# Values in uneven groups around the blocks of the second layer, and one load of v placed later

## The chip, the cores and the metric

The kernel runs on one core of one Trainium2 chip. What counts is the time of the whole execution on the device, in microseconds. Before the change it was 451.67 us, the median of 3 runs (449.34 to 451.85).

The engines are named as in the profile: PE multiplies matrices and writes PSUM, with PEld for the loads of its weights; DVE is VectorE, ACT is ScalarE, POOL is GpSimd, SP is SyncE, which here only issues transfers.

## The reference

Attention with a sigmoid in place of a softmax, and then a layer that works on a chosen part of the tokens. Batch 8, 12 heads, 448 tokens, head size 64, all float32:

```
scores = q @ k^T / 8 - log(448)
attn   = sigmoid(scores) @ v                     # per head
x      = attn of the 12 heads side by side       # (8, 448, 768)
score  = x @ w_gate
for each batch: top = the 128 tokens of highest score
    xe  = x[top]
    out = x;  out[top] = xe + sigmoid(score[top]) * (relu(xe @ w1) @ w2)
```

w1 is 768x1024 and w2 is 1024x768.

## The kernel before

**Steps and slots.** The 96 heads are worked on in 12 steps (s = 0 to 11) of 8 heads. A step has 7 slots (n = 0 to 6), and a slot is a share of the keys: n selects 2 times 32 tokens of keys for each of four head groups. In a slot, `slot` (L738) makes the scores of (s, n), and beside them values (scores times v) of earlier slots. The values run four slots behind: those of step s begin in slot 4 of step s and end in slot 3 of step s + 1.

**Units.** One call of `score(s, n, e, pr, out)` (L330) multiplies on the rows of the array that belong to pr: pr = 1 takes rows 64 to 127, pr = 0 takes rows 0 to 63. Two calls, e = 0 and 1, complete one tile PA[pr] of PSUM, and `squash` (L344) then makes its sigmoid on ACT. One call of `value(s, half, p, n)` (L358) multiplies the sigmoids of slot n with v and adds into the two banks PO[half]; half = 0 uses rows 0 to 63, half = 1 rows 64 to 127. The index p says which of the two banks takes which rows; for each half there are p = 0 and 1 and n = 0 to 6, 14 value units in a step. So a score unit of pr = 1 and a value unit of half = 0 use different rows of the array and run side by side, and likewise pr = 0 and half = 1. I call two units side by side a pair. PE starts its products in the order of the program.

**A plain slot** is, in order: score e0 pr1, two values of half 0, score e1 pr1, sigmoid of PA[1]; then score e0 pr0, two values of half 1, score e1 pr0, sigmoid of PA[0]. That is four pairs. `rounds` (L718) lists which values (p, u, w) stand in which slot; both halves take the same.

**The split slot.** One slot of each step, chosen by `split` (L728), has values of both p of one slot n: in the steps ahead of a block it is the last slot (i = 6, which is slot 3 of the next step). There the order is value half 0, `join(0)`, value half 1, `join(1)`, the four score units, value half 1, value half 0, and the two sigmoids. `join(x)` (L374) is two copies of one element on ACT into the banks PO[x]; the later values of the other p wait for them.

**Blocks.** Behind slot 3 of step s, `after` (L852) loads the next v (`load_v`, L133, four transfers on ACT's queue for s > 4) and calls `block(s)` (L680) for s = 4 to 11. A block moves the finished values out of PSUM (`takes`, DVE transposes, L389) and does the work of the second layer that is listed in `BLOCKS` (L650): "c" chooses the rows of a batch and issues their gather, "t" turns the gathered rows (L524 on PE, then the copies L526 and L527 and a small sigmoid L529 on ACT), and (m, pair, key) is one product of the first (m = 1, 24 records at L560) or second (m = 2, 8 records at L624) matrix, with its sums on DVE and ACT. The banks that these write are handed out in the order of the list `places`:

```
places = [PA[1][:, 0], PO[0][0], PO[0][1], PA[0][:, 0], PO[1][0], PO[1][1], PA[0][:, 0]]
```

A "t" takes two. Blocks 5, 7, 8, 10 and 11 end with a "t", whose second copy empties the seventh place, PA[0]. Block 5 is: choose batch 1, turn batch 0, two products of the first matrix, turn batch 1.

**The order of everything** is written out by hand; each engine works its own list in order, and waits where a tile is not ready. DVE's list holds, between blocks, the transposes of q and k, the gates (L397, L400), sums of weights (L208), and the ranking of tokens (L445, L448) with what follows it (L460, L469, L473).

**v** has one buffer for most steps, so a load of v can start only behind the last values of the step before. It is four transfers of 224 KB, one for each 32 rows; the value unit of half 0 needs the first two, that of half 1 the last two.

Of the kernel before, what the change touches and what calls it, by code (L numbers as in the profile page):

```python
# [17 lines left out]
def kernel(  # L18
# [20 lines left out]
    NF = 3  # L39
# [3 lines left out]
    NS = NQ // 2  # L43
    NU = 2 * NF + 1
# [27 lines left out]
    PA = [ps_a.tile([P, 2, 512], F32, name=f"a{n}") for n in range(2)]  # L72
# [60 lines left out]
    def load_v(s):  # L133


        if s >= NS:
            return
        if s in (1, 3):
            t = moe.tile([P, 6 * KH * P], F32, name="rows_t")[:, :4 * NU * Dh]
        else:  # L140
            t = vals.tile([P, 4 * NU * Dh], F32, name="raw_v")
        raw_v[s] = t = t.rearrange("p (h c) -> p h c", h=4)

        def block(x, r, n):
            return bass.AP(tensor=v.tensor,
                           offset=v.offset + (8 * s + 4 * x) * S * Dh + r * Dh,
                           ap=[[TB * Dh, TT], [S * Dh, 4], [1, n * Dh]])

        for m in range(4):
            y, odd = divmod(m, 2)  # L150
            rows = slice(m * TT, (m + 1) * TT)
            if s:
                (nc.scalar if s > 4 else nc.sync).dma_start(
                    out=t[rows], in_=block(y, odd * NU, NU))
            else:
                nc.sync.dma_start(out=t[rows, :, :NA * Dh], in_=block(y, odd * NA, NA))
                nc.sync.dma_start(out=t[rows, :, NA * Dh:],
                                  in_=block(1 - y, 2 * NA + 2 * odd, 2))
# [215 lines left out]
    def join(x):  # L374

        for t in PO[x]:
            nc.scalar.activation(t[Dh:Dh + 1, S:S + 1], bias_s[Dh:Dh + 1], AF.Copy)

    def takes(s, x):
        for pr in range(2):  # L380
            take(s, pr, x)
# [130 lines left out]
    def turn_rows(b, both):  # L512


        n = CAP
        p, odd = divmod(b, 2)
        if not odd:
            t = moe.tile([P, 6 * KH * P], F32, name="rows_t")
            pairs[p] = {"x": t.rearrange("p (m k n) -> p m k n", m=6, k=KH)}
        x = pairs[p]["x"]  # L520
        ps = [t.rearrange("p (k n) -> p k n", n=P) for t in both]
        for t in range(KD):
            a, i = divmod(t, KH)
            nc.tensor.transpose(ps[a][:, i, :n], st[b]["xe"][:n, t * P:(t + 1) * P],  # L524
                                iden[:n, :n])
        nc.scalar.activation(x[:, 2 * odd, :, :n], ps[0][:, :KH, :n], AF.Copy)  # L526
        nc.scalar.activation(x[:, 2 * odd + 1, :, :n], ps[1][:, :KH, :n], AF.Copy)  # L527
        st[b]["gate"] = moe.tile([P, 1], F32, name="gate", bufs=4)
        nc.scalar.activation(st[b]["gate"][:n], st[b]["picked"][:n], AF.Sigmoid)  # L529
        if not odd:  # L530
            return
        for dst, y, z in ((4, 2, 0), (5, 3, 4), (2, 3, 2)):
            nc.vector.tensor_tensor(out=x[:, dst, :, :n], in0=x[:, y, :, :n],
                                    in1=x[:, z, :, :n], op=ALU.subtract)
        pairs[p]["turned"] = True
        last_row(p)
# [143 lines left out]
    def block(s):  # L680

        places = [PA[1][:, 0], PO[0][0], PO[0][1], PA[0][:, 0], PO[1][0], PO[1][1], PA[0][:, 0]]
        work = BLOCKS.get(s, ())
        if work and work[0][0] == "c":
            chosen = choose(work[0][1], places.pop(0))
        takes(s - 1, 0)
        if work and work[0][0] == "c":
            fetch(*chosen)
            work = work[1:]
        takes(s - 1, 1)  # L690
        stores(s, NF)
        if s in FULL[::2]:
            gates(2 * s - 2)
        for item in work:
            if item[0] == "t":
                turn_rows(item[1], [places.pop(0) for _ in range(2)])
            elif item[0] == "c":
                fetch(*choose(item[1], places.pop(0)))
            else:
                finish(item, begin(item, places.pop(0)))  # L700
# [17 lines left out]
    def rounds(s):  # L718


        if s == 0:
            return [(0, 0, 1), (1, 0, 1), (1, 0, 1), (0, 0, 1), (0, 4, 5), (0, 1, 6), (1, 4, 5)]
        same = [(0, 0, 1), (1, 0, 1), (1, 2, 3), (0, 2, 3), (0, 4, 5)]
        if s + 1 in BLOCKS:
            return same + [(1, 4, 5), (1, 0, 6)]
        return same + [(0, 1, 6), (1, 4, 5)]

    def split(s, i):  # L728
        return i == (6 if s + 1 in BLOCKS else 5)

    def entries(s, i, half):

        p, u, w = rounds(s)[i]
        if s == 0 and i < 4 and (i < 2) == bool(half):
            u, w = 2, 3
        return (p, u), (p, w)

    def slot(s, n):  # L738


        if s == 0 and n < NF + 1:
            if n == NF:
                first_outs.close()
                open_outs()
            psc = PA if n % 2 else outs
            for e in range(2):
                for pr in (1, 0):
                    score(s, n, e, pr, psc[pr])
            for pr in (1, 0):
                squash(s, n, pr, psc[pr])  # L750
            return
        vs, i = (s, n - NF - 1) if n > NF else (s - 1, n + NF)
        if split(vs, i):
            one, two, u = rounds(vs)[i]
            for half in range(2):
                value(vs, half, one, u)
                join(half)
            for e in range(2):
                for pr in (1, 0):
                    score(s, n, e, pr, PA[pr])  # L760
            for half in (1, 0):
                value(vs, half, two, u)
            for pr in (1, 0):
                squash(s, n, pr, PA[pr])
            return
        for half in range(2):
            pr = 1 - half
            a, b = entries(vs, i, half)
            if s == 0 and n == NF + 1 and half == 0:
                value(vs, half, *a)  # L770
                value(vs, half, *b)
                score(s, n, 0, pr, PA[pr])
            else:
                score(s, n, 0, pr, PA[pr])
                value(vs, half, *a)
                value(vs, half, *b)
            score(s, n, 1, pr, PA[pr])
            if vs == 0 and half == 1 and i in (1, 3):
                join(1 if i == 1 else 0)
            squash(s, n, pr, PA[pr])  # L780
            if i == 6 and s not in BLOCKS:
                takes(vs, half)
# [69 lines left out]
    def after(s, n):  # L852

        if n == NF and s:
            odd = s in FULL[1::2]
            if s > 4:
                load_v(s)
            elif s < 4:
                load_v(s + 1)
            if s in BLOCKS:  # L860
                block(s)
            else:
                stores(s, n)
            if s == 2:
                gates(2 * s - 2)
            turn("q", 2 * s + 2)
            turn("k", 2 * s + 3)
            load("k", 2 * s + 4)
            turn("q", 2 * s + 3)
            if s not in FULL[::2]:  # L870
                gates(2 * s - 2)
            if s == FIRST:
                ranking(1)
            gates(2 * s - 1)
        for m, key, place in LENT.get((s, n), ()):
            lend(m, key, place)
        if s == 0:
            if n == 0:
                turn("k", 1)
                turn("q", 1)  # L880
                load("k", 2, 3)
                load("q", 2, 3)
            if n == 4:
                turn("k", 2, 3)
                load_v(1)
                load("k", 4)
            if n == 5:
                turn("q", 2, 3)
        if (s, n) in WEIGHTS:
            m, x = WEIGHTS[s, n]  # L890
            if x is None:
                load_left(m)
            else:
                load_held(m, x)
        for m, key in KEPT.get((s, n), ()):
            keep_sum(m, key)
        if (s, n) in MADE:
            make_sum(*MADE[s, n])
        for b in range(B - 1):
            full = FULL[b]  # L900
            if (s, n) == ((4, 0) if b == 1 else (full, 5 + b % 2)):
                spread(b)
            if (s, n) == RANKED[b]:
                ranking(b)
        if n != NF:
            stores(s, n)
# [63 lines left out]
```

## Time and profile before

| | |
|---|---|
| median of 3 runs | 451.67 us (449.34 to 451.85) |
| the profiled execution | 450.95 us |
| its span, first to last instruction | 449.1 us |
| PE busy | 437.2 us, 97% |
| DVE, ACT, POOL busy | 301.8, 191.0, 32.7 us |
| mean granted clock of PE | 0.989 |
| one score product (L339), one value product (L368) | 538 ns, 536 ns; eight run at a time |
| one sigmoid (L353) | 1007 ns |
| 24 products of the first matrix at full clock | 2.68 us |

Times in the trace count from the span's start. The products of PE overlap, so a sum of their durations says little; what a stretch takes is read from the starts. PE shows each float32 product of this kernel's slots as two records. A share of busy time near 100% does not mean that the array is full: a score unit alone on its rows keeps PE busy and half of the array empty.

### The profile page before, as it was taken

How to read it: one execution, taken by the hardware profiler on the slowest of the kernel's cores; microseconds unless marked ns; L12 is line 12 of the kernel's file. 1: busy time of each engine (PE TensorE's matmuls, PEld its weight loads, DVE VectorE, ACT ScalarE, POOL GpSimd, SP SyncE). 2: the span in 40 equal slices, each digit the busy share in tenths (PEclk: the TensorE clock that was granted, in tenths of full speed). 3: DMA queues.
4: the chain of work that ended last, by engine and by line, in shares of the span. 5: the costliest groups of instructions: out<-in, count | busy, mean ns of one | idle time of the engine just before them, and what ended most of it. 6: DMA issues, size and time to landing. Idle time of an engine off the chain costs nothing.

```text
span 449.1 us, 14350 instructions
## 1 busy us (share of the span) xinstructions
PE 437.2 (97%) x6374; PEld 259.9 (58%) x6374; DVE 301.8 (67%) x639; ACT 191.0 (43%) x257; POOL 32.7 (7%) x55
## 2 busy tenths in 40 slices
PE   8999999999989999999999999999999999999994
PEld 3456554444358568446447558636545749769952
DVE  4317277945954995966998785655795669883462
ACT  4766666665643641660661661462264330101100
POOL 7000000000001000100002000010000101001001
PEclk9999999999988999999999999999999999999998
DMA  8975737997571898679566499399864974611001
GB/s 242 257 239 132 259 86 141 233 222 177 163 210 43 181 325 218 178 203 312 165 225 159 131 249 191 84 265 227 223 229 85 203 224 64 118 36 72 1 0 70
DMA packets 112846, 76.80 MB, mean 171 GB/s; under 512 B 90304, under 2 KB 99136, under 8 KB 112784
## 3 DMA queue, kind: packets, MB, share of 16 engines
q1 hardware_dynamic: 106768, 61.55, 53.0%
q10 hardware_dynamic: 4032, 6.42, 6.2%
q0 software_dynamic: 1984, 7.91, 5.9%
q8 instruction: 50, 0.82, 0.8%
q14 instruction: 12, 0.10, 0.1%
HBM read 55.41 MB, written 20.46 MB: 169 GB/s over the span
## 4 chain that ended last, share of the span: by engine, by line
PE 86%; DVE 8%; ACT 2%; issue 2%; DMA 1%; ACTq 1%; POOLq 0%; DVEq 0%
PE a L339 27%; PE o L368 23%; PE o L624 12%; PE o L560 10%; PE a L560 7%; PE a L624 3%; DVE scr L448 1%; DVE scr L445 1%; ACT attn L353 1%; PE p L926 1%; ACT hidden L353 1%; DVE x_b L389 1%; DVE sums L473 1%; DVE spare L208 1%; DVE kT L321 1%
## 5 line engine op out<-in xcount | busy, mean ns | idle before, releaser
L339 PE MATMUL a<-qT,kT 32*64 32x448 f32 x2624 | 244.4, 538 | 0.6 <-DVE got L496 0.5
L353 ACT ACTIVATE attn<-a,bias_s 128x896 f32<-128x896 f32 x162 | 161.9, 1007 | 84.8 <-PE a L339 81.1
L368 PE MATMUL o<-attn,raw_v 32*64 32x448 f32 x2176 | 197.3, 536 | 0.1
L339 PEld LDWEIGHTS a<-qT,kT 32*64 32x64 f32 x2624 | 92.6, 131 | 96.8 <-ACT attn L353 57.3
L368 PEld LDWEIGHTS o<-attn,raw_v 32*64 32x64 f32 x2176 | 74.3, 131 | 31.3 <-issue 24.5
L389 DVE STREAM_TRANSPOSE x_b<-o 128x448 f32<-128x448 f32 x48 | 27.6, 620 | 55.3 <-PE o L368 32.5
L368 PE MATMUL o<-attn,rows_t 32*64 32x448 f32 x448 | 42.3, 537 | 0.1
L576 ACT ACTIVATE hidden<-hidden 128x512 f32<-128x512 f32 x12 | 7.5, 630 | 70.1 <-DVE hidden L573 70.1
L400 DVE TENSOR_REDUCE gate_p<-scr 128x14 f32<-128x448 f32 x48 | 29.8, 622 | 1.7
L573 DVE TENSOR_TENSOR hidden<-o,hidden 128x512 f32<-128x512 f32 x20 | 13.2, 687 | 25.4 <-PE o L560 25.2
L397 DVE TENSOR_TENSOR scr<-x_b,wg_b 128x448 f32<-128x448 f32 x48 | 29.4, 612 | 1.1
L321 DVE STREAM_TRANSPOSE kT<-raw_k 128x448 f32<-128x448 f32 x42 | 24.1, 612 | 8.2 <-PE o L368 4.5
L624 PE MATMUL o<-w_sb,hidden 128*128 128x384 f32 x80 | 27.4, 487 | 0.0
L635 DVE SCALAR_TENSOR_TENSOR xe<-o,gate,xe 128x384 f32<-128x384 f32 x36 | 20.5, 611 | 9.5 <-PE o L624 9.3
L313 DVE STREAM_TRANSPOSE qT<-qT 128x896 f32<-128x896 f32 x23 | 25.0, 1085 | 2.7 <-DMA qT<-in_q_dram 2.7
L560 PE MATMUL o<-rows_t,w_sb 128*128 128x128 f32 x192 | 23.2, 278 | 0.0
L526 ACT ACTIVATE rows_t<-o 128x384 f32<-128x384 f32 x7 | 3.4, 483 | 45.9 <-PE o L524 43.6
L560 PEld LDWEIGHTS o<-rows_t,w_sb 128*128 128x128 f32 x192 | 22.7, 196 | 0.3
L448 DVE SCALAR_TENSOR_TENSOR scr<-rep,who,earlier 128x448 f32<-128x448 f32 (+1 forms) x32 | 21.9, 683 | 1.4
L445 DVE TENSOR_SCALAR_CACHE_REDUCE scr<-rep,who 128x448 f32<-128x448 f32 (+1 forms) x32 | 21.5, 673 | 1.0
L368 PEld LDWEIGHTS o<-attn,rows_t 32*64 32x64 f32 x448 | 17.6, 131 | 6.4 <-issue 4.6
L624 PEld LDWEIGHTS o<-w_sb,hidden 128*128 128x128 f32 x80 | 14.7, 190 | 8.8
(114 smaller groups left out, 403.1 us busy)
## 6 DMA issues: line engine op xcount, KB each, us to landing
qT<-in_q_dram SPq DMA_DIRECT2D x24, 448.0 KB, 6.2
out_dram<-x_b SPq DMA_DIRECT2D x32, 336.0 KB, 8.6
raw_k<-in_k_dram SPq DMA_DIRECT2D x22, 448.0 KB, 5.3
spare<-sum SPq DMA_DIRECT2D x18, 384.0 KB, 5.2
raw_v<-in_v_dram ACTq DMA_DIRECT2D x28, 224.0 KB, 6.1
sum<-spare SPq DMA_DIRECT2D x8, 768.0 KB, 7.2
w_sb<-in_moe_w_dram SPq DMA_DIRECT2D x6, 768.0 KB, 7.6
rows_t<-in_v_dram SPq DMA_DIRECT2D x8, 224.0 KB, 5.9
```

What stands on the lines that cost most here:

```text
L313: nc.vector.transpose(heads["q", i], heads["q", i])
L321: nc.vector.transpose(kt[:, e], t[:, e].rearrange("p (a n) d -> p n a d", a=2))
L339: nc.tensor.matmul(out[y * Dh:(y + 1) * Dh, h % 2, :S], kt[d, e, r:r + 2].rearrange("d r t -> d (r t)"), qt[d, e], start=(e == 0), stop=(e ...
L353: nc.scalar.activation(a, psc[:, :, :S], AF.Sigmoid, bias=bias_s, scale=QK_SCALE)
L368: nc.tensor.matmul(PO[x][pr][j * Dh:(j + 1) * Dh, :S], raw_v[s][rows, 2 * pr + j, at:at + Dh], attn[s, pr, n][rows, j, :], start=((s, x, p ...
L389: nc.vector.transpose(x_tiles[b][:, :, 2 * g + pr, :], PO[x][pr][:, :S].rearrange("p (r t) -> p r t", t=TT))
L397: nc.vector.tensor_tensor(out=tmp, in0=x_tiles[b][:, :, hp, :], in1=wg_b[:, hp:hp + 1, :].to_broadcast([P, TB, TT]), op=ALU.mult)
L400: nc.vector.tensor_reduce(out=gate_parts[b][:, :, hp], in_=tmp, axis=AX.X, op=ALU.add)
L445: nc.vector.tensor_scalar(out=junk[:n], in0=rep[:n], scalar1=own, scalar2=0.0, op0=ALU.is_gt, op1=ALU.add, accum_out=above[:n, c:c + 1])
L448: nc.vector.scalar_tensor_tensor(out=junk[:n], in0=rep[:n], scalar=own, in1=earlier[:n, c, :], op0=ALU.is_equal, op1=ALU.mult, accum_out=l ...
L560: nc.tensor.matmul(ps[:, f, :n], w((t * FH + f) * P, P), x[:, t, :n], start=(t == 0), stop=(t == KH - 1))
L624: nc.tensor.matmul(ps[:n, :DH], h[:, t, :n], w(t * DH, DH), start=(t == 0), stop=(t == FH - 1))
```

## The change

It does four things. The first three hold for the values of steps 4 to 10, called `LATE`; the values of other steps are placed as before.

1. The two halves no longer take the same values in a slot. `LOW` and `HIGH` list them by slot, for half 0 and half 1.
2. The first two slots behind a block (slots 4 and 5) are written out in `first_slots`. In slot 4 the second score unit of PA[1] and the first of PA[0] stand side by side, in the second pair, so that PA[1] is complete after the second pair and PA[0] after the third, and the fourth pair holds two values. Half 0 has one value of each p there, with `join(0)` between.
3. The last slot before the next block is written out in `last_slot`, and replaces the split slot: its first pair holds two values, PA[1] is complete after the third pair and PA[0] after the fourth. Half 0 is finished after the second pair, half 1 after the fourth, with `join(1)` between its two values.
4. The four transfers of v for step 5 are issued in block 5 behind the row turn of batch 0 (behind L529 on ACT's queue) instead of ahead of the block.

The number of products, sigmoids, copies and transfers is the same, and so is the order on DVE, SP and POOL. The core of the diff:

```
@@ block(s)
             if item[0] == "t":
                 turn_rows(item[1], [places.pop(0) for _ in range(2)])
+                if item[1] == 0:
+                    load_v(s)
@@
+    LATE = range(min(BLOCKS), NS - 1)
+    LOW = {6: (1, 3, 4), 0: (0, 1, 2), 1: (1, 5, 6), 2: (0, 3, 4), 3: (0, 5, 6)}
+    HIGH = {6: (1, 0, 1), 0: (1, 2, 3), 1: (1, 4, 5), 2: (0, 4, 5)}
+
+    def first_slots(s, n):
+        def u(e, pr):
+            score(s, n, e, pr, PA[pr])
+
+        if n == NF + 1:
+            u(0, 1)
+            value(s, 0, 0, 0)
+            join(0)
+            u(1, 1)
+            u(0, 0)
+            squash(s, n, 1, PA[1])
+            value(s, 1, 0, 0)
+            u(1, 0)
+            squash(s, n, 0, PA[0])
+            value(s, 1, 0, 1)
+            value(s, 0, 1, 0)
+            return
+        u(0, 1)
+        value(s, 0, 1, 1)
+        value(s, 0, 1, 2)
+        u(1, 1)
+        squash(s, n, 1, PA[1])
+        u(0, 0)
+        value(s, 1, 0, 2)
+        value(s, 1, 0, 3)
+        u(1, 0)
+        squash(s, n, 0, PA[0])
+
+    def last_slot(s, n):
+        p, one, two = LOW[n]
+        value(s - 1, 1, 0, NU - 1)
+        value(s - 1, 0, p, one)
+        join(1)
+        score(s, n, 0, 1, PA[1])
+        value(s - 1, 0, p, two)
+        score(s, n, 1, 1, PA[1])
+        score(s, n, 0, 0, PA[0])
+        squash(s, n, 1, PA[1])
+        value(s - 1, 1, 1, NU - 1)
+        score(s, n, 1, 0, PA[0])
+        squash(s, n, 0, PA[0])
@@ entries(s, i, half)
+        if s in LATE:
+            p, u, w = (HIGH if half else LOW)[(i + NF + 1) % NU]
+            return (p, u), (p, w)
@@ slot(s, n)
-        if split(vs, i):
+        if vs in LATE and i < 2:
+            first_slots(s, n)
+            return
+        if vs in LATE and n == NF:
+            last_slot(s, n)
+            return
+        if vs not in LATE and split(vs, i):
@@ after(s, n)
-            if s > 4:
+            if s > 5:
                 load_v(s)
```

## The prediction

> **What bounds the kernel now.** TensorE does. The page's first row has PE busy 97% of the 449.1 us span, and the chain that ended last is 86% PE. So a change gains only where PE waits, where it runs without its partner, or where its clock is low. I read three views for that. First the page's slices, for the granted clock:
>
> ```profile
>
> ```
>
> One place inside the kernel, slices 12 and 13 of 11.2 us each, is below full. The waits of PE name what stands there:
>
> ```profile
> PE a L560 <- ACT rows_t L526: 1.5, 1, 1.5
> ```
>
> It is the longest wait of PE. The chain in order of time shows it (start, us, what), and from the next block a product of the same size:
>
> ```profile
> 129.09 0.39 ACTq L153
> ...
> 130.00 1.15 ACTq L153
> ...
> 131.81 0.50 ACT rows_t L526
> ...
> 132.36 5.49 PE a L560 x24
> ...
> 170.23 2.68 PE a L560 x24
> ```
>
> In the block of step 5, ScalarE issues the four transfers of v (L153, 129.09 to 131.63) ahead of the copy that PE needs (L526). Then 24 products take 5.49 us instead of 2.68. The windows give the reason (PE busy first, PEclk after the five engines):
>
> ```profile
> 131.00:132.00 1.00, 0.00 (x0) 0.00 (x0) 1.00 (x2) 0.19 (x1) 0.57 (x1) 0.86 1.08 245
> 132.00:133.00 1.00, 0.64 (x3) 0.65 (x4) 0.93 (x3) 0.77 (x3) 0.00 (x0) 0.50 1.09 232
> ...
> 138.00:139.00 1.00, 1.00 (x9) 1.00 (x8) 0.00 (x0) 0.48 (x1) 0.58 (x1) 0.72 0.00 0
> 139.00:140.00 1.00, 1.00 (x12) 1.00 (x11) 0.00 (x0) 0.00 (x0) 0.00 (x0) 1.00 0.40 108
> ```
>
> By the shares 0.86 and 0.72 the clock is half from 131.72 to 138.55, 6.83 us. PE works from 132.36, so half speed costs (138.55 - 132.36) / 2 = 3.1 us on top of the wait.
>
> **The units.** In the timeline a score unit is 8 records, a value unit 8, and one of each run side by side in 0.75 us; a slot is four such pairs, 3.02 us. I write t0 for the start of the last slot before a block and E for the first score behind it.
>
> **Last slot (blocks 5 to 11).** Before, it takes 3.85 us (159.84 to 163.69 in step 6), since scores and values run unpaired and one score waits. The weight loads show it:
>
> ```profile
> 160.63 0.18 PEld L339 LDWEIGHTS a<-qT,kT 32*64 32x64 f32 x4 [0.20 <-issue]
> 161.27 0.58 PEld L339 LDWEIGHTS a<-qT,kT 32*64 32x64 f32 x20 [0.46 <-ACT attn L353]
> ```
>
> After, four full pairs end at t0 + 3.1. But the block's first product writes PA[1], whose last score pair is now the third. A sigmoid starts 0.75 after its second round (159.47, then 160.21): t0 + 1.9 + 0.75 = 2.65; it takes 1.01, and PE follows 0.05 later: t0 + 3.70. So 0.15 is gained, not 0.75. The two small ScalarE copies that each new join adds to a slot (0.25 us by L377's 0.44 for four) stand ahead of a sigmoid; only a value a pair or more later waits for them, and before there were four per last slot. I cost them at nothing, at most 0.25 each.
>
> In blocks 9 and 11 the next wait, for VectorE's transposes of PO[0] (L389), also goes: PO[0] is complete after the second pair, so both transposes (0.65 and 0.61) end near t0 + 3.0. The next product starts at 3.70 + 0.36 (choice, 270.41 to 270.77) + 0.19 = t0 + 4.25, instead of 4.72 and 4.67: **-0.47 and -0.42**. Blocks 7 and 10 start with a product in PA[1]: **-0.15 each**. Blocks 6 and 8 gain nothing, because VectorE is late by itself. Its chain runs without a gap from 155.67, and from 213.53, to:
>
> ```profile
> 166.15 0.66 DVE x_b L389
> ...
> 166.85 0.61 PE o L482 x4
> ```
>
> and to 236.20 in block 8. Its order is not changed.
>
> **Block 5.** Before: t0 = 125.07, E = 141.51, so 16.44. After: choice at t0 + 3.70, for 0.91 (128.93 to 129.84); row turns at 4.61; the first copy 0.53 after them (213.32, 213.85 in block 7), at 5.14, for 0.49; PE 0.06 later at 5.70, not 7.29. Two products at 2.68 and six turns at 0.75 give E = t0 + 11.81 at full clock: **-4.63**, of which 3.1 is the clock.
>
> The moved step is four issues on ScalarE's queue, now behind L529 at about t0 + 6.15. They take 1.75 (four at 0.44) to 2.55 us. Behind them stands L579, wanted at t0 + 8.45; it is 0.25 late at most, and its reader comes 2.7 us later. No other queue is passed. What is new is when v lands. Before, the last piece lands 7.95 after the first issue (137.04); other blocks show 7.3 to 12.3. That is t0 + 13.4 to 18.4, wanted at E + 1.69 = 13.5. The lower end is 0, the upper 4.9. I take 0, because nothing but the gather was moving beside it before, and the 1.15 of the third issue included a wait for a weight that landed at 130.47, which is past by then.
>
> **First slots behind a block.** The first score of PA[0] moves from the third pair to the second, from E + 1.55 to E + 0.8. PA[0] is the last bank that a row turn used in blocks 5, 7, 8 and 10. Its copy ends at E + 0.65 in blocks 7 and 10: nothing. In blocks 5 and 8 a relu stands in front:
>
> ```profile
> 248.48 0.63 ACT L576 ACTIVATE hidden<-hidden 128x512 f32<-128x512 f32 x1 [2.88 <-DVE hidden L573]
> 249.02 0.47 ACT L526 ACTIVATE rows_t<-o 128x384 f32<-128x384 f32 x1
> 249.39 0.48 ACT L527 ACTIVATE rows_t<-a 128x384 f32<-128x384 f32 x1
> ```
>
> It ends at E + 1.63 (E = 248.24). The score starts at E + 1.69, its partner has gone alone, and one pair of the next slot loses its partner: the two slots last 6.95, against 3.24 + 3.02 before. **+0.7 in each of blocks 5 and 8.** Between, the groups only change which values stand in a slot; every slot has four pairs, and each value's sigmoid is at least a slot old: 0.
>
> **Sum.** -4.63 + 0.7 + 0.7 - 0.15 - 0.15 - 0.47 - 0.42 = -4.4. The profiled execution took 450.95 (span 449.1), so it would take 446.5. The median of the runs shown, 451.67, stands 0.7 above it, so I predict **447.2**. The lowest of them, 449.34, is 2.3 lower, which fits an execution without the half clock; from there the other terms, -1.3, give 448.0.
>
> **A rule on the clock.** The row: the slow stretch is 6.83 us, and in the 3.4 us ahead of it PE was still recorded busy for about 2.6 us (idle only from 130.9). [...] The row says that a thin window is enough, so 449.6 stays possible.
>
> **Rivals.**
> *The half clock stays.* Between the last pair and block 5's first product there are still 2.6 us (t0 + 3.1 to 5.7) of small work, against 3.4 before. If that is thin enough, at an unlucky time, 3.1 comes back: 449.6, or 450.3 beside the median. For it: 104.94 to 106.91 is as thin for 2.0 us and kept full clock, so the limit lies somewhere between 2.0 and 3.4. [...] 0.17.
> *v lands late in step 5* (slower). From the seventh microsecond after the first issue PE stands at the third value unit; at the trace's longest, 12.3, it stands 4.9, and the idle time brings the half clock, 3.1 more: 446.5 + 0.7 + 8.0 = 455.2. For it: the gather of 384 KB shares the engines, whose share is 0.72 to 1.26 from 130 to 135.5. Against: no other transfer is issued from 124.2 to 135.9. 0.08.
> *It does not do what it says:* the pairs of the new slots fall out of step at all seven blocks as in 5 and 8, 0.7 each, five more: 447.2 + 3.5 = 450.7. Against: the margins in 7 and 10 are 0.1, but 6 and 9 free PA[0] long before. 0.09.
>
> **The numbers.** The forecast gets 0.66, own range 445.4 to 448.6 (the small terms doubled or gone, the two bases). The range, 445.4 to 450.9, takes in the half clock and the lost pairs. 1% is 4.5 us, about what a measurement of this kernel can tell from no change: faster by more means below 447.15, which the forecast's middle touches: 0.42 (nearly two thirds of the forecast's chance, since the profiled execution's own sum lies below). Slower by more means above 456.2, late v with a second slow stretch, or several of these cases at once: 0.07. Within: 0.51.
>
> **What would show it.** Right: no L153 ahead of L526 in block 5, the first 24 products in 2.7 us, PEclk full throughout; last slots of 3.1 us with a wait on a sigmoid (L353) behind; a wait of some 0.9 us on the second copy of the row turn behind blocks 5 and 8; blocks 6 and 8 still ending a VectorE wait. Wrong: a half clock anywhere, or PE waiting for a transfer of v behind block 5.

## The result: 446.36 us after 451.67, ratio 0.9896

| | before | after |
|---|---|---|
| median, 5 executions each | 451.67 us (449.34 to 452.33) | 446.36 us (445.79 to 446.79) |
| ratio, 95% interval | | 0.9896 [0.9865, 0.9927] |
| the profiled execution | 450.95 us | 446.79 us |
| its span | 449.1 us | 445.0 us |
| PE busy | 437.2 us | 430.2 us |
| mean granted clock | 0.989 | 0.997 |

The forecast, 447.2, is 0.8 above the median, and its range held it. The median lies below 447.15, the outcome to which the prediction gave 0.42, but the interval lies on both sides of it. Since one term of the sum failed, the other small terms gained more than forecast, and an accident that is no part of the change hid that in the profiled execution, the way there needs more telling than the number.

The PEclk row of the slices (the granted clock, one digit for each 11.2 us) before:

```profile
PEclk9999999999988999999999999999999999999998
```

and after:

```profile
PEclk9999999999999999999999999999999999999998
```

The two eights in slices 12 and 13 are gone. The waits of PE in the profile after (total, times, longest, in us):

```profile
...
PE a L560 <- ACT attn L353: 1.2, 3, 0.4
PE a L482 <- ACT attn L353: 1.0, 3, 0.4
...
PE o L368 <- issue: 0.6, 2, 0.4
...
PE a L560 <- ACT rows_t L526: 0.3, 1, 0.3
```

The wait for the row copy (L526) fell from 1.5 to 0.3. What is late next there is the sigmoid ahead of a block (L353, six waits), as forecast. The last "issue" row is the accident, told below. The chain in order of time, in block 5 after the change (start, us, what):

```profile
128.89 0.45 issue
129.34 1.02 PE a L486 x8
...
130.79 0.50 ACT rows_t L526
...
131.33 2.94 PE a L560 x24
134.28 2.68 PE o L560 x24
```

No L153 stands in it; the first product takes 2.94 us, not 5.49. The windows of the same place (PE first, PEclk after the five engines, then the DMA share and GB/s) show why:

```profile
131.00:132.00 1.00, 0.75 (x7) 0.67 (x7) 1.00 (x3) 0.75 (x3) 0.88 (x1) 1.00 0.00 0
132.00:133.00 1.00, 1.00 (x12) 1.00 (x11) 0.96 (x2) 0.00 (x0) 0.00 (x0) 1.00 0.56 118
```

**Where the time went.** I read the starts of PE's products in both traces. E with a block's number is the first score behind that block, as in the prediction.

| stretch | before | after | difference | forecast |
|---|---|---|---|---|
| E4 to E5 (last slot, block 5) | 34.60 | 29.96 | -4.64 | -4.63 |
| E5 to E6 | 36.69 | 36.69 | 0.00 | +0.7 |
| E6 to E7 | 35.87 | 35.63 | -0.24 | -0.15 |
| E7 to E8 | 34.16 | 34.18 | +0.02 | 0 |
| E8 to E9 | 36.56 | 36.45 | -0.11 | +0.7 - 0.47 |
| E9 to E10 | 35.87 | 36.67 | +0.80 | -0.15 |
| E10 to E11 | 34.13 | 33.47 | -0.66 | -0.42 |
| E11 to the end | 94.35 | 94.36 | +0.01 | 0 |
| sum | 342.23 | 337.43 | -4.80 | -4.4 |

The spans differ by 4.13 us, 0.67 less than this sum: in the execution after, PE reached E4 that much later (107.58, before 106.91), in code that the change does not touch.

### The profile page after: what moved, and what is told of

It reads as the page before. It is cut to its first block, busy times and chain, and to the rows that moved or that the text cites. A ratio compares the mean times of both kernels' runs of the same rounds, so it can differ in the third digit from the quotient of the medians.

```text
span 445.0 us, 14349 instructions
## 1 busy us (share of the span) xinstructions
PE 430.2 (97%) x6374; PEld 259.2 (58%) x6374; DVE 302.6 (68%) x639; ACT 191.2 (43%) x257; POOL 32.8 (7%) x55
## 4 chain that ended last, share of the span: by engine, by line
PE 88%; DVE 5%; ACT 3%; issue 1%; DMA 1%; POOLq 0%; ACTq 0%; DVEq 0%
PE a L339 27%; PE o L368 25%; PE o L624 12%; PE o L560 10%; PE a L560 7%; PE a L624 4%; ACT attn L353 2%; PE p L989 1%; DVE spare L208 1%; PE p L339 1%; DMA out_dram<-xe,idx 1%; ACT hidden L353 1%; DVE scr L448 1%; DVE scr L445 1%; DVE scr L397 1%
## 5 line engine op out<-in xcount | busy, mean ns | idle before, releaser
L353 ACT ACTIVATE attn<-a,bias_s 128x896 f32<-128x896 f32 x162 | 161.4, 1007 | 83.8 <-PE a L339 79.8
L368 PE MATMUL o<-attn,raw_v 32*64 32x448 f32 x2176 | 194.6, 536 | 0.5 <-issue 0.4
L400 DVE TENSOR_REDUCE gate_p<-scr 128x14 f32<-128x448 f32 x48 | 29.8, 622 | 1.7
L573 DVE TENSOR_TENSOR hidden<-o,hidden 128x512 f32<-128x512 f32 x20 | 13.3, 688 | 21.1 <-PE o L560 20.9
L526 ACT ACTIVATE rows_t<-o 128x384 f32<-128x384 f32 x7 | 3.4, 484 | 43.9 <-PE o L524 43.9
```

The lines of the kernel that those rows point to most:

```text
L353: nc.scalar.activation(a, psc[:, :, :S], AF.Sigmoid, bias=bias_s, scale=QK_SCALE)
L368: nc.tensor.matmul(PO[x][pr][j * Dh:(j + 1) * Dh, :S], raw_v[s][rows, 2 * pr + j, at:at + Dh], attn[s, pr, n][rows, j, :], start=((s, x, p ...
L400: nc.vector.tensor_reduce(out=gate_parts[b][:, :, hp], in_=tmp, axis=AX.X, op=ALU.add)
```

## The experiments

My theory: the gain is block 5, through the wait for the four issues and the half clock behind it; a thin stretch of PE sets the half clock, not the transfers; behind blocks 5 and 8 a relu that stands ahead of the row copies costs 0.7 us each. Rivals: the clock falls for another reason that stands beside the wait; the uneven groups, not the load, carry the gain; late v is dear.

### One part alone

The load alone, on the kernel before:

```
             if item[0] == "t":
                 turn_rows(item[1], [places.pop(0) for _ in range(2)])
+                if item[1] == 0:
+                    load_v(s)
...
-            if s > 4:
+            if s > 5:
                 load_v(s)
```

> The kernel before with the later load of v in step 5 alone; its last slots and first slots are those of before. Theory (the wait of the copies and the half clock behind it are one cost, and the move takes both away): the copies follow the row turn, so block 5 loses 1.5 us of waiting and, where the half clock had come, 3.1 more; no execution shows a granted clock under full in the middle. Against the executions of before that have the half clock 4.6 less, about 447.1; against those without it 1.5 less. Rival (the first product is slow for its own sake, because its weights or its rows are still being moved): 1.5 less in every execution, about 450, and the product still takes 5.5 us.

Measured: 448.28 us, ratio 0.9898 [0.9848, 0.9947]. Block 5 takes 8.23 us from its first product to E, where before took 12.58, so 4.35 less; the clock is full there, 0.996 over the whole execution. Its profile has a long stall that no part of the edit explains:

```profile
PE o L368 <- issue: 1.8, 2, 1.3
```

The stretch with the stall, E6 to E7, is 1.78 longer than before; the others behind block 5 are those of before within 0.04. So the load carries the gain of block 5, all but 0.3.

The groups alone, with v ahead of the block again:

```
-                if item[1] == 0:
-                    load_v(s)
...
-            if s > 5:
+            if s > 4:
                 load_v(s)
```

> The kernel after with the load of v in step 5 put back ahead of the block, so the uneven groups alone. Theory: the copies of block 5 wait for the four issues as before, and the half clock can come; of the other parts +0.7 in block 8, -0.2 in 7 and 10, -0.7 in 9, -0.4 in 11 remain, about -0.8 against before: 450.9 with the half clock, 448.5 without. Rival (the groups are what makes the gain): about 446.5 to 447.5 in every execution.

Measured: 448.84 us, ratio 0.9922 [0.989, 0.9955]. The wait in its profile is longer than before, since PE is there earlier and ACT's queue is not:

```profile
PE a L560 <- ACT rows_t L526: 2.2, 1, 2.2
```

and the clock is half again, for 6.83 us. From E4 to the end it is 1.03 below before, close to the -0.8 of the forecast's terms. Its median is some 2 us lower than this would give, and near the 448.5 that was expected for executions without the half clock; its ten mean clocks, 0.986 to 0.998, say that some had none. (Its profiled execution, 454.15 at a mean clock of 0.986, is its slowest and had a second half clock near its start, from 13.29 for 3.41 us, so only stretches are read from it.) That the parts' medians add up to more than the whole, about -4.6 and -3.5 by their ratios against -4.7, stays open.

### The half clock

Two kernels pull the wait and the clock apart. The first keeps the load and its wait as before, and gives PE twelve products of no use behind the row turn, so that the stretch is full:

```
                 turn_rows(item[1], [places.pop(0) for _ in range(2)])
+                if item[1] == 0:
+                    for _ in range(12):
+                        nc.tensor.matmul(PA[0][:, 0, :P], iden, iden, start=True, stop=True)
```

> The kernel before, with 12 products of 128 columns added on PE behind the row turn of batch 0 in block 5, into a bank that the next product overwrites; the four issues and the wait of the copies stay. Theory (the clock falls because the 3.4 us are thin): PE stays full of work, the clock stays full, the first product takes 2.7 us at the old place; 3.1 less than executions of before with the half clock, about 448.6. Rival (not the thin stretch): the time of before, 451.7, with a product of 5.5 us.

Measured: 450.6 us, ratio 0.9963 [0.9937, 0.9989], a mean clock of 0.996 to 0.999 in all ten executions (25 of before on the same chip: 0.985 to 0.995). Its timeline (start, us, engine, line):

```profile
130.81 2.84 PE L699 MATMUL a<-iden 128*128 128x128 f32 x24
133.49 2.73 PE L560 MATMUL a<-rows_t,w_sb 128*128 128x128 f32 x23
```

and windows at the place where before had 0.50, with the transfers beside it as before:

```profile
132.00:133.00 1.00, 1.00 (x11) 1.00 (x11) 0.93 (x3) 0.95 (x3) 0.00 (x0) 1.00 0.96 206
133.00:134.00 1.00, 1.00 (x11) 1.00 (x11) 0.96 (x2) 0.01 (x1) 0.00 (x0) 1.00 1.15 274
```

From the first product of the first matrix to E it takes 6.10 us (133.49 to 139.59), where before takes 9.15 (132.36 to 141.51): 3.05 less, the forecast's 3.1. The whole block takes 10.58, 2.00 less than before, because the added products let that first product start 1.04 later. By its median the kernel gains 1.4 us, where 3.1 were expected against executions with the half clock; the later start takes 1.0 of them, and the rest is not shown. So more work made the kernel faster, and the clock's price is shown by itself.

The second takes the changed kernel, where v comes late, and makes the stretch thin with four activations of no use ahead of the copies:

```
+                    for _ in range(4):
+                        pad = moe.tile([P, S], F32, name="scr")
+                        nc.scalar.activation(pad, earlier[:, 0, :], AF.Copy)
                 turn_rows(item[1], [places.pop(0) for _ in range(2)])
```

> The kernel after, with four small activations of ScalarE (448 columns each, of no use) ahead of the copies of the first row turn in block 5, so that the copies come some 1.5 us later and the thin stretch of PE is as long as before, but with no transfer issued in it. Theory (a long thin stretch brings the half clock): in most executions 1.5 + 3.1 more than after, about 451; where the clock stays full, 1.5 more, 447.9. Rival (the issues of the transfers slow the product): 1.5 more in every execution, 447.9, with a product of 2.7 us.

Measured: 454.07 us, ratio 1.0047 [1.0023, 1.0071]. The wait is longer than meant, because the pads' tile is one that DVE was still reading (ACT stood 4.33 us until L400 was done with it):

```profile
133.91 2.40 ACT L699 ACTIVATE scr<-earlier 128x448 f32<-128x448 uint8 x4 [4.33 <-DVE gate_p L400]
136.22 0.47 ACT L526 ACTIVATE rows_t<-o 128x384 f32<-128x384 f32 x1
136.25 0.39 ACTq L153 DMA_DIRECT2D raw_v<-in_v_dram  x1
```

The clock falls at 132.36, more than 3 us before the first piece of v is issued (136.25), and it is half also in a microsecond in which no transfer moves anything:

```profile
134.00:135.00 1.00, 0.00 (x0) 0.00 (x0) 0.89 (x6) 0.97 (x2) 0.00 (x0) 0.50 0.00 0
```

It stayed half until 142.60, 10.24 us in all, and all ten executions have a mean clock of 0.985 to 0.992. So a thin stretch suffices and the load of v is not needed. The size missed, for the reason given.

Before has 3.29 us of thin work between its last pair and block 5's first product (129.07 to 132.36 in the chain), and by the mean clocks, 0.985 to 0.998, took the half clock in most of its executions, not in all. After has 2.44 (128.89 to 131.33) and never showed it: the 14 executions of it and of its repeat have 0.996 and above, and the profiled executions of the three kernels that the section on blocks 5 and 8 tells of, with the same code up to there, have 0.996 to 0.998. What a stretch between these two lengths does is not shown.

### What a moved load costs

v issued another 3.7 us later, behind the end of block 5's first product (L579):

```
-                if item[1] == 0:
-                    load_v(s)
...
                 finish(item, begin(item, places.pop(0)))
+                if item == (1, 0, 1):
+                    load_v(s)
```

> The kernel after with the four transfers of v for step 5 issued 3.7 us later still, behind the copy of the first product (L579). The slower rival of the prediction, made to happen: the second piece lands 3 us behind the end of block 5, the two slots behind it lose 2.7 us more than in after, of which block 6 gives back 0.6 where PE waited for VectorE: 2.0 more than after. If the idle PE brings the half clock in some executions, up to 3 us more in those. If PE waits for the four pieces less than 2 us, v lands faster when less stands beside it.

Measured: 446.97 us, ratio 0.9903 [0.9869, 0.9938], beside 446.67 for the changed kernel on the same chip: +0.3, which is inside the spread of either. PE did wait for v (timeline of weight loads, the idle time in front and its releaser at the end):

```profile
139.30 0.13 PEld L368 LDWEIGHTS o<-attn,raw_v 32*64 32x64 f32 x2 [0.75 <-DMA raw_v<-in_v_dram]
...
141.30 0.13 PEld L368 LDWEIGHTS o<-attn,raw_v 32*64 32x64 f32 x2 [0.53 <-DMA raw_v<-in_v_dram]
```

The stretch from E5 to E6 grew by 0.62, not by the 2 expected: the second piece landed 3.85 us after its issue, where it takes 5.23 in the changed kernel with the gather beside it; that the gather makes the difference was expected, and is not shown. No half clock followed (PEclk 1.00 in each microsecond from 138 to 142); PE ran scores between the waits. In the changed kernel the last piece lands at 138.88, and PE comes for it when the second row copy releases it:

```profile
139.24 0.21 PEld L339 LDWEIGHTS a<-qT,kT 32*64 32x64 f32 x8 [0.75 <-ACT rows_t L527]
```

The values that read v follow 0.1 behind that score. So the load has some 0.4 us to spare, and costs nothing there.

### The slots behind blocks 5 and 8

After block 5, ACT's timeline shows the forecast's queue:

```profile
137.80 0.63 ACT L576 ACTIVATE hidden<-hidden 128x512 f32<-128x512 f32 x1 [2.89 <-DVE hidden L573]
138.34 0.47 ACT L526 ACTIVATE rows_t<-o 128x384 f32<-128x384 f32 x1
138.71 0.48 ACT L527 ACTIVATE rows_t<-a 128x384 f32<-128x384 f32 x1
```

I first moved all of the product's end, DVE's sum (L573) and ACT's relu, behind the row turn, in block 5 and in block 8:

```
-                finish(item, begin(item, places.pop(0)))
+                args = begin(item, places.pop(0))
+                after_it = work[work.index(item) + 1:][:1]
+                if s in (5,) and after_it and after_it[0][0] == "t":
+                    held.append((item, args))
+                else:
+                    finish(item, args)
...
                 turn_rows(item[1], [places.pop(0) for _ in range(2)])
+                while held:
+                    finish(*held.pop())
```

(The second kernel has 8 in place of 5.)

> The kernel after, with the sums and the relu of the last product of block 5 issued behind the copies of the row turn, not ahead of them. PA[0] is then free 0.6 us earlier and the 0.64 us that the two slots behind block 5 lose should be gone. Theory A (what the profiles of before and after show: from the end of block 5 to the end of block 6 both take 36.7 us, since VectorE's list runs without a gap in between and PE waits for it in block 6): the gain is lost again in block 6, 0 to 0.1 in all, 446.4 beside after's 446.4. Theory B (the sum of the prediction: the slots' loss counts in full): 0.65 less, 445.7.

> The same edit in block 8 alone. From the end of block 8 to block 9 PE is not waiting for VectorE, so by theory A as by theory B the 0.61 us of the two slots behind block 8 go: 0.6 less than after, 445.8. If neither slot gets shorter, the wait was not the relu's.

Measured: 447.87 us, 0.9921 [0.9886, 0.9957], and 448.31 us, 0.9934 [0.9903, 0.9965]. Both missed. PE's weight loads behind block 5 of the first:

```profile
140.23 0.15 PEld L368 LDWEIGHTS o<-attn,raw_v 32*64 32x64 f32 x4 [2.18 <-DVE hidden L573]
```

and DVE's timeline of the same kernel:

```profile
137.42 1.69 DVE L533 TENSOR_TENSOR rows_t<-rows_t 128x384 f32<-128x384 f32 x3 [0.84 <-ACT rows_t L526]
...
139.49 0.69 DVE L573 TENSOR_TENSOR hidden<-o,hidden 128x512 f32<-128x512 f32 x1
```

The sum reads a bank that a value writes next, and I had put it behind 2.1 us of row subtractions. Behind block 8 the same wait, 2.18 us, stands in the second. The two slots grew by 1.3 us in each, in place of shrinking. (In the first, E5 to E6 grew by 2.49 in all: its profile also has a stall of 1.5 us ahead of block 6, of the kind told in the last section.) These runs do not test the relu; they test a wait of my own.

So I moved the relu alone (blocks 5, 8, 11) and left the sum where it was:

```
             add(h[0], ps, h[2])
-            relu(h[0])
+            if hold is None:
+                relu(h[0])
+            else:
+                hold.append(h[0])
...
                 turn_rows(item[1], [places.pop(0) for _ in range(2)])
+                while held:
+                    h = held.pop()
+                    nc.scalar.activation(h, h, AF.Relu)
```

> The kernel after with the relu of the last product of blocks 5, 8 and 11 behind the copies of the row turn; the sum on VectorE that reads the product's bank stays ahead, unlike in the two kernels before. The copies then end near E + 0.65, as behind blocks 7 and 10, and the two slots behind blocks 5 and 8 take 6.07 in place of 6.89. Block 8: 0.8 less. Block 11: 0.15 less. Block 5, theory A (VectorE's list sets block 6): 0.8 is gone from the slots, but only what VectorE's list starts earlier stays, about 0.5; theory B: 0.8. In all 1.45 less than after by A, 1.75 by B.

Measured: 444.58 us, ratio 0.9857 [0.9818, 0.9896], 2.1 below the changed kernel's run beside it. Its ACT timeline has the copies first:

```profile
137.39 0.49 ACT L526 ACTIVATE rows_t<-o 128x384 f32<-128x384 f32 x1 [2.46 <-PE o L524]
137.78 0.49 ACT L527 ACTIVATE rows_t<-a 128x384 f32<-128x384 f32 x1
...
138.24 0.63 ACT L703 ACTIVATE hidden<-hidden 128x512 f32<-128x512 f32 x1
```

E5 to E6 falls by 0.95, E8 to E9 by 0.86, and E11 to the end by 0.22. The first two are more than the 0.64 and 0.61 that PE had lost between E and the last slot, because the slots there are now 0.24 shorter than before the change (18.09 us from E to the last slot, before 18.33, after 18.97 and 18.94). That block 6 lets the gain of block 5 pass, DVE explains:

```profile
137.91 1.69 DVE L533 TENSOR_TENSOR rows_t<-rows_t 128x384 f32<-128x384 f32 x3
```

The row subtraction starts at E5 + 0.35. In the changed kernel it waits for the copy until E5 + 1.30 (138.84), and before it did so until E5 + 1.29 (142.80):

```profile
142.80 1.69 DVE L533 TENSOR_TENSOR rows_t<-rows_t 128x384 f32<-128x384 f32 x3 [1.07 <-ACT rows_t L526]
```

From it DVE's list runs to the transposes in block 6, which come at E5 + 24.64 before, E5 + 24.65 after, and E5 + 23.70 with the relu moved. So the copy behind block 5 sets when DVE reaches block 6. Theories A and B were both too small in block 5, and since DVE's list and the slots moved by nearly the same, this run does not part them; before and after do, below.

### The heads of blocks, the repeat, and the best of them

After the change, six waits for a sigmoid stand ahead of blocks, because PA[1] is the first place that a block writes. Here blocks 5, 7, 9, 10 and 11 take PO[0] first, and its transposes go ahead of the choice:

```
+        early = s in (5, 7, 9, 10, 11)
+        if early:
+            places[:3] = places[1], places[2], places[0]
+            takes(s - 1, 0)
...
-        takes(s - 1, 0)
+        if not early:
+            takes(s - 1, 0)
```

> The kernel after, with the banks of blocks 5, 7, 9, 10 and 11 handed out in another order: PO[0][0] and PO[0][1] first, PA[1] third, and the transposes of PO[0] ahead of the choice. PE then does not wait for the last sigmoid of PA[1] at the head of these blocks. Theory (the wait of 0.45 to 0.55 us at each head is that sigmoid's and nothing else is late there, as the transposes end at t0 + 3.0): heads at t0 + 3.1 in place of 3.6, five times 0.5, 2.5 less than after, 443.9. Rival (the transposes of VectorE are late next): less than 1 us gained.

Measured: 444.93 us, ratio 0.9865 [0.9824, 0.9905]. The stretches ahead of blocks 5, 7, 9 and 11 shrink against after by 0.49, 0.46, 0.37 and 0.24, 1.6 us together and not 2.5; block 10 gains nothing against the other kernels (35.62, beside 35.64 in the groups alone). Its waits show the sigmoid down from 1.2 and 1.0 to:

```profile
PE a L560 <- ACT attn L353: 0.3, 1, 0.3
PE a L482 <- ACT attn L353: 0.3, 1, 0.3
```

With it, and the failed move of sum and relu in blocks 5, 8 and 11:

> The edits of the two before and of the places together, the relu behind the copies in blocks 5, 8 and 11. By theory A: 2.5 for the heads, 0.6 in block 8 and up to 0.2 in block 11, about 443.2; by theory B 0.65 less again, 442.5.

Measured: 449.35 us, ratio 0.9963 [0.9936, 0.9991]: the wait for L573 again, in three blocks, a miss of the same make.

The changed kernel once more, as the measure for the last four:

> The kernel after as it is, beside the three others on the same chip, so that differences of half a microsecond can be read. About 446.4 to 447.9, full clock in the middle of every execution.

Measured: 446.67 us, ratio 0.9902 [0.9873, 0.9932], which repeats the result.

The relu alone and the places together:

> That edit and the other order of the banks at the heads of blocks 5, 7, 9, 10 and 11 together: 2.5 and 1.45 less than after, about 4 us; theory: the two do not touch each other.

Measured: 441.64 us, ratio 0.9806 [0.9762, 0.9851]. It beats both kernels, by 5.0 us the changed one beside it. From E4 to the end it takes 332.52 us: 4.91 less than after, of which 1.0 is the accident told below, so 3.9, the 4 that were expected.

## Why the prediction was right, and where it was wrong

**Block 5: right, in each part.** Forecast -4.63, measured -4.64. The choice came at t0 + 3.67 (forecast 3.70), the first product at t0 + 5.66 (5.70), E at t0 + 11.87 (11.81). That 3.1 of it is the clock was argued; the filled stretch shows 3.05.

**The half clock as a rival.** It did not come; that the thin stretch brings it, and not the load's traffic, is shown from both sides: 0.996 to 0.999 with the stretch filled, 0.985 to 0.992 with it made longer. After still has 2.44 us of thin work there, where before has 3.29, so how near it was is not shown.

**v lands late, the slower rival: its price fell.** The forecast's own value, nothing, was right: the last piece lands 7.63 after the first issue (7.95 before), not 12.3. With the load another 3.7 us later PE waited 0.75 and 0.53 us for it, E5 to E6 grew by 0.62, and the clock stayed full. The rival's price of 8 us, of which 3.1 were the clock, had taken the longest landing of other blocks, and had counted a wait between scores like a stretch of small work. One of its reasons is not shown: it put the 1.15 us of the third issue down to a weight that landed at 130.47, but in the filled kernel the third issue takes 1.30 us (130.08 to 131.38) and nothing lands in it. In after all four issues take 0.44 or less.

**+0.7 in each of blocks 5 and 8.** The mechanism was right: the two slots last 6.89 and 6.87 us (forecast 6.95), the wait on the second copy stands where it was said to, 0.75 us long. In block 8 the stretch carries the loss: +0.61 from E to the last slot. **In block 5 the step failed**: E5 to E6 is the same to 0.01, in the groups alone and with the pads too (36.68 and 36.69). PE lost 0.64 in the slots and won 0.28 in the last slot, so it came to block 6 about 0.35 later, and there a wait for DVE took it up. The weight loads of the choice in block 6 before:

```profile
166.85 0.52 PEld L482 LDWEIGHTS o<-ones,sums 128*128 128x128 f32 x4 [0.41 <-DVE x_b L389]
```

and after:

```profile
162.89 0.52 PEld L482 LDWEIGHTS o<-ones,sums 128*128 128x128 f32 x4
```

The wait of 0.41 is gone. The prediction had itself written that block 6 is set by DVE, and used it for the gain, as nothing; it did not use it for the loss, which vanishes in the same wait. It had also read DVE's chain back only to 155.67, not to the copy behind block 5 where it starts.

**Blocks 7, 9, 10, 11: mechanism right, sizes small.** -0.24, -0.72, -0.24 (below) and -0.66 where -0.15, -0.47, -0.15 and -0.42 stood. In block 9 the choice comes at t0 + 3.56, the next product at t0 + 4.03, forecast 3.70 and 4.25: the sigmoid started at t0 + 2.50, and the forecast had taken 2.65 from an unpaired slot; the choice's 0.36 + 0.19 were 0.47.

**Blocks 6 and 8 gain nothing: right.** E7 to E8 is +0.02.

**An accident evened it out.** The small terms together were +0.2 by the forecast and -1.2 by the table without E9 to E10's excess. In the profiled execution PE then stood about 1.0 us in step 10, between two products of one value unit that wait for no engine:

```profile
296.42 0.13 PEld L368 LDWEIGHTS o<-attn,raw_v 32*64 32x64 f32 x1 [0.24 <-issue]
297.38 0.14 PEld L368 LDWEIGHTS o<-attn,raw_v 32*64 32x64 f32 x3 [0.83 <-issue]
```

Where this is absent (the groups alone, the relu alone, the later v) the slots from E9 to block 10 take 21.78 us, not 22.82. So -4.64 - 1.2 + 1.0 = -4.8, beside -4.4: two misses, of 1.4 and 1.0 us, in opposite directions. The median's -4.7 by the ratio is near both by some luck as well, because the half clock of before does not seem to be in all of its executions: of 16 on one chip (one more, at 455.98, stands apart), the five with a mean clock of 0.996 or more took 448.7 to 451.4 us, the eleven others 450.8 to 454.6.

**Pairs out of step everywhere:** did not happen; the two slots behind blocks 6, 7, 9 and 10 take 6.06 us in all, and took 6.06 to 6.08 before.

## What to carry to other kernels

Where PE runs thin, as here for 3.29 us, count the clock behind it as well as the wait; 3.1 of the 4.6 us were clock, and useless products won 2.0 of that block back. A term on PE has to be carried to the next place where PE waits for another engine: up to the length of that wait a loss costs nothing there, as a gain wins nothing (here a wait of 0.41 us in block 6 took up a loss of about 0.35). Before an operation is moved down a queue, ask of each tile that it reads who writes it next: moving a sum with its relu lost 1.3 us behind block 8, where moving the relu alone won 0.86.

## What the runs showed that was not expected

PE stands "for issue" in some executions. Stalls of 0.8 to 1.8 us between starts of neighbouring products appear in the profiles of after (step 10), its repeat (steps 7 and 10), the load alone (step 7), and both kernels with the sum moved (ahead of block 6, and in step 10), and none of that size in those of before, the relu alone or the best kernel. Each ends 1.3 to 1.5 us after a packet of 16,384 bytes on the queue of kind "instruction" has passed:

| kernel | packet at, us | it takes | stall ends |
|---|---|---|---|
| after | 294.86 | 0.98 | 297.38 |
| after again | 186.03 | 1.05 | 188.35 |
| after again | 296.44 | 0.99 | 298.94 |
| load alone | 186.27 | 1.03 | 188.80 |
| sum and relu moved, block 5 | 159.01 | 0.99 | 161.48 |
| sum and relu moved, block 8 | 296.80 | 0.99 | 299.15 |

The page of every kernel has 50 such packets, so most pass without a stall. Whether the packet has to do with the stall no run tried; it stays open.
